# Moving two matmuls behind a Winograd product, and swapping the two column halves of the last one

## The chip, the cores and the metric

The kernel runs on one core of one Trainium2 chip. The metric is device time in microseconds of one launch. Three runs of the kernel before gave 194.7, 194.7 and 194.68 us (median 194.7). A separate execution, taken with the hardware profiler, gave the page and the trace used below; its own time is 194.69 us, and 192.9 us of it lie between its first and its last instruction (the span). The TensorE clock granted in that execution was 1.0 of full speed throughout.

## The reference

A retention layer (linear attention with a decay per head) feeds a two-layer perceptron with the Mish activation, `h * tanh(softplus(h))`.

```python
for t in range(S):                       # B=4, H=8, S=768, D=64
    state = gamma * state + outer(k[:, :, t], v[:, :, t])
    y[:, :, t] = scale * (q[:, :, t] @ state)
x = y.transpose(0, 2, 1, 3).reshape(B * S, H * D)      # 3072 tokens x 512
h = x @ w_in                                            # 512 -> 2048
g = h * tanh(softplus(h))
out = g @ w_out                                         # 2048 -> 512, float32
```

## The kernel before

The recurrence is computed in chunks of 128 tokens; 24 chunks make the 3072 tokens. The chunks are grouped into 11 blocks: block 0 has four chunks (512 tokens), blocks 1 to 10 have two (256 tokens). The order of instructions on each engine is written out by hand, and each engine works through its own list in that order. An instruction starts when the semaphores that it waits for have been reached; what stands behind a waiting instruction on the same engine waits with it. (TensorE has two rows in the trace, PE for the matmuls and PEld for the loads of their stationary operand; a load may run while the matmul before it runs.)

For each of the blocks 4 to 10 the program calls `mixed_in` and then `seven`. Both use a Winograd form: a 2x2 by 2x2 block product with seven block multiplications in place of eight, with sums and differences of blocks made ahead by VectorE (DVE).

`mixed_in` makes the first product, `h = x @ w_in`, transposed: 128 features by 256 tokens at a time, 16 such feature groups. Eight of the groups (0 to 3 and 8 to 11) are made by seven Winograd products; each is a call of `mm` (its matmul is L857) with eight matmuls that move 128 columns. The other eight groups (4 to 7 and 12 to 15) are made plainly; four calls of `plain` (matmul on L877) make two groups each, with eight matmuls that move 256 columns: for each of the two groups four steps over the 512 inputs, which add up in one half of a PSUM bank. Products and plain calls take turns. The results go through

- `kept` (L887), a ScalarE (ACT) copy of a PSUM bank to SBUF,
- `plus` (L892), a DVE addition of a PSUM bank and such a copy,
- `mish` (L868), the ACT activation that writes the block's `g`, 128x512 at a time.

The last part of `mixed_in` is, in order of PE: the product `mm(pf, s(4), b[1][1])`; the third plain call, groups 12 and 13, into the bank of the pool `pxps` (call it po); the product `mm(pa, s(3), t[2])`, "third product" below, which adds onto the bank pa; the fourth plain call, groups 14 and 15, into the bank ph; and `mm(pa, a(1,1), t[3])`, "last product" below, which adds onto the same bank pa once more. Between the last two uses of pa DVE has to read it: `h22 = plus(pa, m5)`. The bank pa can be written again only when that addition has read it.

ACT's last five activations of `mixed_in` are, in this order: h12 (from DVE), po, h22 (from DVE), ph, and pa after the last product.

`seven` makes the block's `out = g @ w_out` for two tiles of 128 tokens, 512 columns in two halves of `hf` = 256, by seven products of eight matmuls each (L951; `mm` of `seven`). Its first product reads groups 0 to 7 of `g`; its second reads groups 12 to 15 and then 8 to 11, of which those of the token half in question are written by the last activation of `mixed_in`, that of pa. `snap` (L957) is an ACT copy from PSUM, `done` (L964 copy, L966 addition) the DVE step that makes a finished part of the output tile; in the last block each `done` is followed at once by a DMA (L968) on the SP queue, in other blocks the stores are issued later.

In `seven` of the last block the last product `mm(.., a(1, 1), t(4))` is cut into two column halves of 128. The half 0 to 127 adds onto the bank px, which by then holds the sum `u3`; it is finished by a copy. The half 128 to 255 is made in a fresh bank pl; it is finished by an addition of the part of `u3` that ACT copied out earlier (`snap(px, ...)`). Before px is written again, the addition `done(1, 1, px, m5)` must have read it.

Of the kernel before, what the change touches and what calls it, by code (L numbers as in the profile page):

```python
# [16 lines left out]
def kernel(  # L17
# [9 lines left out]
    nc = tc.nc  # L27
    B, H, S, D = q.shape
    d_model, d_ff = moe_w_in.shape
    P = 128  # L30
    C = 128
# [8 lines left out]
    NBP = d_model // P  # L40
# [805 lines left out]
    def mixed_in(blk, last):  # L846

        b, t = x_views(blk)
        n = NFB // 4
        gt = gtiles[blk, 0] = gp.tile([P, NFB, 2 * C], FP16, name="g", tag="g", bufs=3)  # L850
        for f in range(NFB):
            gts[blk, f] = gt[:, f]

        def mm(o_ps, w, x, begin=False):
            for f in range(n):
                for k in range(2):
                    nc.tensor.matmul(  # L857
                        o_ps[:, f], w(f // 2, k)[:, f % 2 * P:(f % 2 + 1) * P], x[:, k],
                        start=begin and f == 0 and k == 0, stop=k == 1, skip_group_check=True)

        def a(i, j):
            return lambda h, k: wins[2 * i][h][:, 2 * j + k]

        def s(i):
            return lambda h, k: wsums[h][:, i - 1, k]

        def mish(to, src):
            nc.scalar.activation(to, src, AF.Mish, scale=inv_boost3)  # L868

        def part(i, j):  # L870
            return gt[:, i * 2 * n:i * 2 * n + n, j * C:(j + 1) * C]

        def plain(h_ps, f0):
            for f in range(2):
                w, h = divmod(f0 + f, n)
                for k in range(NBP):
                    nc.tensor.matmul(  # L877
                        h_ps[:, f], wins[w][h // 2][:, k, h % 2 * P:(h % 2 + 1) * P],
                        xts[blk][:, k, :2 * C], start=k == 0, stop=k == NBP - 1)
            return lambda: mish(gt[:, f0:f0 + 2], h_ps)  # L880

        def bank(pool, tag, whole=False):
            return pool.tile([P, 2, 2 * C] if whole else [P, n, C], FP32, name="h_ps", tag=tag)

        def kept(o_ps):
            m = op.tile([P, n, C], FP32, name="hsum", tag="hsum", bufs=6)
            nc.scalar.copy(m, o_ps)  # L887
            return m

        def plus(x, y):  # L890
            m = op.tile([P, n, C], FP32, name="hsum", tag="hsum", bufs=6)
            nc.vector.tensor_tensor(m, x, y, op=ALU.add)  # L892
            return m

        pp = bank(mmps, "mm", True)
        pf = bank(mmps, "mm")
        pa = bank(mmps, "mm")
        mm(pa, a(0, 0), b[0][0], True)
        m1 = kept(pa)
        plain(pp, n)()  # L900
        mm(pf, s(1), t[0], True)
        m5 = kept(pf)
        if not last:
            settle(blk + 1)
            mask_two(blk + 1)
        plain(bank(pxps, "px", True), n + 2)()
        pm = bank(mmps, "mm")
        mm(pm, a(0, 1), b[1][0], True)
        h11 = plus(pm, m1)
        mm(pa, s(2), t[1])  # L910
        u2 = kept(pa)
        mish(part(0, 0), h11)
        mm(pf, s(4), b[1][1])
        h12 = plus(pf, u2)
        mish(part(0, 1), h12)
        plain(bank(pxps, "px", True), 3 * n)()
        mm(pa, s(3), t[2])
        h22 = plus(pa, m5)
        mish(part(1, 1), h22)
        if not last:  # L920
            leave(blk + 1)
        sums_a(blk, 0)
        ph = atps.tile([P, 2, 2, 2 * C], FP32, name="h_ps", tag="at")[:, 0]
        plain(ph, 3 * n + 2)()
        mm(pa, a(1, 1), t[3])
        mish(part(1, 0), pa)
        sums_a(blk, 1)

    def seven(blk, masks, hooks, last):
        n, hf = NFB // 2, d_model // 2  # L930
        px = pxps.tile([P, hf], FP32, name="o_ps", tag="px")
        pb = mmps.tile([P, hf], FP32, name="o_ps", tag="mm")
        osb = [
            op.tile([P, d_model], FP32, name="osb", tag="osb") for _ in range(2)]

        def a(i, j):
            return lambda f: gts[blk, j * n + f][:, i * P:(i + 1) * P]

        def b(i, j):
            return lambda f: wouts[(i * n + f) // FPS][:, f % FPS, j * hf:(j + 1) * hf]  # L940

        def s(i):
            return lambda f: gsums[blk % 2][:, i - 1, f]

        def t(i):
            return lambda f: tmats[(i - 1) // 2][:, (i - 1) % 2, f]

        def mm(o_ps, x, w, first=False, turn=0, part=slice(None), cols=slice(None)):
            for z in range(n)[part]:
                f = (z + turn) % n  # L950
                nc.tensor.matmul(  # L951
                    o_ps[:, cols], x(f), w(f)[:, cols], start=first and z == 0, stop=z == n - 1,
                    skip_group_check=True)

        def snap(o_ps, cols=slice(0, hf)):
            x = op.tile([P, hf], FP32, name="snap", tag="snap", bufs=3)[:, cols]
            nc.scalar.copy(x, o_ps[:, cols])  # L957
            return x

        def done(i, j, o_ps, plus=None, cols=slice(0, hf)):  # L960
            at = slice(j * hf + cols.start, j * hf + cols.stop)
            dst = osb[i][:, at]
            if plus is None:
                nc.vector.tensor_copy(dst, o_ps[:, cols])  # L964
            else:
                nc.vector.tensor_tensor(dst, o_ps[:, cols], plus, op=ALU.add)  # L966
            if last:
                nc.sync.dma_start(out_rows(blk, i)[:, at], dst)  # L968

        def call(fns):  # L970
            for fn, *args in fns:
                fn(*args)

        mm(px, a(0, 0), b(0, 0), True)
        m1 = snap(px)
        mm(pb, a(0, 1), b(1, 0), True, n // 2 if blk >= MIX else 0)
        if blk < ONE:
            sums_b(blk)
            if blk == 1:
                cast_behind(blk, 2)  # L980
            sums_c(blk)
            if blk > 1:
                cast_behind(blk, 3)
            done(0, 0, pb, m1)
            call(masks)
        else:
            done(0, 0, pb, m1)
            if blk == ONE:
                call(masks)
            sums_b(blk)  # L990
            if not tight(blk):
                cast_behind(blk, 2)
                sums_c(blk)
        pe = mmps.tile([P, hf], FP32, name="o_ps", tag="mm")
        alone = blk + 2 >= len(BLOCKS)
        if alone:
            mm(px, s(2), t(2))
            u2 = snap(px)
        mm(pe, s(1), t(1), True)
        m5 = snap(pe)  # L1000
        if not alone:
            mm(px, s(2), t(2))
            u2 = snap(px)
        if blk < ONE:
            mm(pe, s(4), b(1, 1))
            call(hooks[0])
            call(hooks[1])
            done(0, 1, pe, u2)
            mm(px, s(3), t(3), part=slice(0, n // 2))
            call(hooks[2][:1])  # L1010
            mm(px, s(3), t(3), part=slice(n // 2, n))
            pl = mmps.tile([P, hf], FP32, name="o_ps", tag="mm")
            u3 = snap(px)
            done(1, 1, px, m5)
            call(hooks[2][1:])
            mm(pl, a(1, 1), t(4), True)
            done(1, 0, pl, u3)
        else:
            call(hooks[0])
            if tight(blk):  # L1020
                sums_c(blk)
                cast_behind(blk, 3)
            call(hooks[1])
            mm(px, s(3), t(3))
            if last:
                pl = mmps.tile([P, hf], FP32, name="o_ps", tag="mm")
                u3 = snap(px, slice(hf // 2, hf))
            done(1, 1, px, m5)
            call(hooks[2])
            mixes = not last and blk + 1 >= MIX  # L1030
            if mixes:
                x_sums(blk + 1, 0)
            mm(pe, s(4), b(1, 1))
            done(0, 1, pe, u2)
            cols = slice(0, hf // 2 if last else hf)
            mm(px, a(1, 1), t(4), cols=cols)
            done(1, 0, px, cols=cols)
            if last:
                cols = slice(hf // 2, hf)
                mm(pl, a(1, 1), t(4), True, cols=cols)  # L1040
                done(1, 0, pl, u3, cols)
            if mixes:
                x_sums(blk + 1, 1)
        if not last:
            for i in range(2):
                stores.append((1 + i, out_rows(blk, i), osb[i]))
# [344 lines left out]
```

## Time and profile before

| | |
|---|---|
| median of three runs | 194.7 us |
| profiled execution, its own time | 194.69 us |
| its span, first to last instruction | 192.9 us |
| PE busy | 188.0 us, 97% of the span |
| DVE busy | 137.4 us, 71% |
| ACT busy | 104.4 us, 54% |
| POOL busy | 74.0 us, 38% |
| one matmul of 256 columns (L877, L951), start to end | 273 ns |
| one matmul of 128 columns (L857), start to end | 219 ns |
| one load of a stationary operand | 98 ns |
| `mish` L868 from PSUM / from SBUF | 587 / 631 ns |
| `plus` L892 | 691 ns |
| DMA of the last block's 64 KB pieces, issue to landing | 1.6 us |

Matmuls are pipelined: the next one starts long before the one in front has ended, so the pace of a group is read from the starts of groups, not from the duration of one. In the timeline a row is a group of equal instructions that follow each other: start in us from the span's start, us from the first start to the last end, engine, line, operation, tiles and shapes, and in brackets the idle time of the engine before it with what ended it. In the chain of waits, which is followed back from the last instruction, a matmul that had to wait a little still counts as PE.

### The profile page before, as it was taken

To read this page: it belongs to the slowest core of one execution; us is meant where nothing else is said; L and a number is where in the kernel's file an instruction comes from. 1 tells how busy PE (TensorE), PEld (TensorE's weight loads), DVE (VectorE), ACT (ScalarE), POOL (GpSimd) and SP (SyncE) were. 2 spreads that over 40 slices of the span, in tenths; PEclk is the share of its full clock that TensorE was granted. 3 is DMA by queue.
4 is the path that set the end of the run, shared out by engine and by line. 5 is a ranking of instruction groups with operands and counts; after the bars stand their busy time and mean duration, and the time that the engine had idled before them with its cause. 6 is when DMAs were issued, how large, how long until landed. Compare 5 with 4: busy or idle time off the path is not lost.

```text
span 192.9 us, 7199 instructions
## 1 busy us (share of the span) xinstructions
PE 188.0 (97%) x3124; PEld 161.5 (84%) x3124; DVE 137.4 (71%) x273; ACT 104.4 (54%) x193; POOL 74.0 (38%) x100
## 2 busy tenths in 40 slices
PE   7999999999999999999999999999999999999993
PEld 7756478888888888888998998998998989988993
DVE  0787469886977877957985884974884894875462
ACT  3375767263643643554584574664763763763850
POOL 5272000577509648733635625715705800000000
PEclk9999999999999999999999999999999999999999
DMA  5999999998999999999999899999896240201202
GB/s 172 305 308 354 383 388 364 291 322 190 197 238 302 188 243 189 185 276 227 211 197 266 191 195 246 169 211 247 106 235 122 51 130 13 103 0 40 77 27 82
DMA packets 83791, 38.78 MB, mean 201 GB/s; under 512 B 57776, under 2 KB 77872, under 8 KB 83760
## 3 DMA queue, kind: packets, MB, share of 16 engines
q1 hardware_dynamic: 83616, 38.28, 86.3%
q8 instruction: 24, 0.39, 0.9%
q10 hardware_dynamic: 144, 0.05, 0.1%
q14 instruction: 7, 0.06, 0.1%
HBM read 27.31 MB, written 6.29 MB: 174 GB/s over the span
## 4 chain that ended last, share of the span: by engine, by line
PE 94%; DMA 3%; DVE 1%; ACT 1%; issue 0%; SPq 0%
PE o_ps L951 32%; PE h_ps L647 17%; PE h_ps L877 13%; PE h_ps L857 12%; PE o_ps L704 7%; PE y_ps L560 3%; DMA qfirst<-in_q_dram 3%; PE u_ps L488 1%; PE at L481 1%; PE t_ps L256 1%; PE y_ps L382 1%; PE h_ps L629 1%; PE at L452 1%; PE at L336 1%; PE u_ps L354 1%; DVE qk L268 1%
## 5 line engine op out<-in xcount | busy, mean ns | idle before, releaser
L647 PE MATMUL h_ps<-xt,win 128*128 128x256 f16 (+1 forms) x272 | 34.3, 285 | 0.0
L951 PEld LDWEIGHTS <-gsum 128*128 128x128 f16 x320 | 30.3, 98 | 3.9
L647 PEld LDWEIGHTS <-win 128*128 128x128 f16 x272 | 26.4, 98 | 6.5 <-DVE win L213 0.2
L656 ACT ACTIVATE g<-h_ps 128x512 f16<-128x512 f32 x38 | 22.7, 597 | 15.9 <-PE h_ps L647 15.9
L951 PE MATMUL o_ps<-tmat,gsum 128*128 128x256 f16 x240 | 29.8, 273 | 0.0
L877 PE MATMUL h_ps<-xt,win 128*128 128x256 f16 x224 | 29.0, 273 | 0.0
L951 PEld LDWEIGHTS <-g 128*128 128x128 f16 x248 | 23.4, 98 | 2.6
L957 ACT COPY snap<-o_ps 128x256 f32<-128x256 f32 (+1 forms) x33 | 12.2, 369 | 20.1 <-PE o_ps L951 20.1
L966 DVE TENSOR_TENSOR osb<-o_ps,snap 128x256 f32<-128x256 f32 (+1 forms) x33 | 13.8, 417 | 12.8 <-PE o_ps L951 9.2
L877 PEld LDWEIGHTS <-win 128*128 128x128 f16 x224 | 20.7, 98 | 1.9
L868 ACT ACTIVATE g<-h_ps 128x512 f16<-128x512 f32 x35 | 19.9, 587 | 3.3 <-PE h_ps L877 3.3
L887 ACT COPY hsum<-h_ps 128x512 f32<-128x512 f32 x21 | 12.3, 585 | 14.8 <-PE h_ps L857 14.8
L423 POOL TENSOR_TENSOR qk<-qf,qvs 128x512 f16<-128x512 f32 x18 | 19.1, 1061 | 2.0 <-DMA qf<-in_q_dram 2.0
L892 DVE TENSOR_TENSOR hsum<-h_ps,hsum 128x512 f32<-128x512 f32 x21 | 14.5, 691 | 7.4 <-PE h_ps L857 5.2
L426 POOL TENSOR_TENSOR qk<-kf,qvs 128x512 f16<-128x512 f32 x18 | 18.9, 1051 | 1.8 <-DMA kf<-in_k_dram 1.8
L433 POOL TENSOR_TENSOR v<-vf,qvs 128x512 f16<-128x512 f32 x18 | 19.1, 1077 | 1.1 <-DMA vf<-in_v_dram 1.0
L951 PE MATMUL o_ps<-wout,g 128*128 128x256 f16 x160 | 19.1, 273 | 0.0
L1289 POOL COPY summed<-gsum 128x1 f16<-128x1 f16 x7 | 2.9, 421 | 34.2 <-DVE gsum L817 24.5
L857 PE MATMUL h_ps<-xt,wsum 128*128 128x128 f16 x224 | 15.9, 219 | 0.0
L609 ACT CAST xt<-y_ps 128x512 f16<-128x512 f32 x15 | 10.2, 734 | 10.2 <-PE y_ps L560 10.2
L857 PEld LDWEIGHTS <-wsum 128*128 128x128 f16 x224 | 14.0, 98 | 0.3
L868 ACT ACTIVATE g<-hsum 128x512 f16<-128x512 f32 x21 | 13.3, 631 | 1.5 <-DVE hsum L892 1.4
(113 smaller groups left out, 298.6 us busy)
## 6 DMA issues: line engine op xcount, KB each, us to landing
kf<-in_k_dram SPq DMA_DIRECT2D x24, 256.0 KB, 5.4
vf<-in_v_dram SPq DMA_DIRECT2D x24, 256.0 KB, 5.5
out_dram<-osb SPq DMA_DIRECT2D x22, 256.0 KB, 2.8
qf<-in_q_dram SPq DMA_DIRECT2D x20, 256.0 KB, 5.3
wt<-in_moe_w_out_dram SPq DMA_DIRECT2D x6, 512.0 KB, 8.4
wi<-in_moe_w_in_dram SPq DMA_DIRECT2D x4, 512.0 KB, 8.4
wi<-in_moe_w_in_dram SPq DMA_DIRECT2D x2, 1024.0 KB, 11.1
qfirst<-in_q_dram SPq DMA_DIRECT2D x2, 512.0 KB, 4.6
```

Of the source, the lines that this page charges most:

```text
L423: nc.gpsimd.tensor_tensor(in_place(q16.rearrange("p (w x) d -> p w x d", x=2)), by_head(qf), scale_by_head(qs_two[:, heads]), op=ALU.mult)
L426: nc.gpsimd.tensor_tensor(k16.rearrange("p (y w) d -> p w y d", y=2), kf.rearrange("p (w y) d -> p w y d", y=2), boosts.rearrange("p (w y) ...
L433: nc.gpsimd.tensor_tensor(cast[g][2], loaded.pop(g)[2], vs[g % 2].unsqueeze(2).broadcast_to((P, H, D)), op=ALU.mult)
L647: nc.tensor.matmul(h_ps[:, j, cols], wins[s][f // 2][:, bp, f % 2 * P:(f % 2 + 1) * P], xts[blk][:, bp, cols], start=(bp == 0 and at == 0) ...
L656: nc.scalar.activation(gt, h_ps, AF.Mish, scale=inv_boost3)
L704: nc.tensor.matmul(banks[ij][:, t], x(f)[:, t * P:(t + 1) * P], w(f), start=ij in open_banks, stop=f == fs[-1], skip_group_check=True)
L857: nc.tensor.matmul(o_ps[:, f], w(f // 2, k)[:, f % 2 * P:(f % 2 + 1) * P], x[:, k], start=begin and f == 0 and k == 0, stop=k == 1, skip_g ...
L868: nc.scalar.activation(to, src, AF.Mish, scale=inv_boost3)
L877: nc.tensor.matmul(h_ps[:, f], wins[w][h // 2][:, k, h % 2 * P:(h % 2 + 1) * P], xts[blk][:, k, :2 * C], start=k == 0, stop=k == NBP - 1)
L892: nc.vector.tensor_tensor(m, x, y, op=ALU.add)
L951: nc.tensor.matmul(o_ps[:, cols], x(f), w(f)[:, cols], start=first and z == 0, stop=z == n - 1, skip_group_check=True)
L966: nc.vector.tensor_tensor(dst, o_ps[:, cols], plus, op=ALU.add)
```

## The change

In `mixed_in`, `plain` gets an argument that says which of its eight steps to issue. The third plain call issues its first six ahead of the third product and its last two behind it. Its activation is still the one that ACT does before that of h22; DVE's and ACT's lists keep their order. This holds for the blocks 4 to 10.

In `seven` of the last block, the half 128 to 255 of the last product (bank pl, finished by an addition) comes first, and the half 0 to 127 (bank px, finished by a copy) second, with their DVE steps and DMAs in the same new order.

```diff
-        def plain(h_ps, f0):
-            for f in range(2):
+        def plain(h_ps, f0, steps=range(2 * NBP)):
+            for step in steps:
+                f, k = divmod(step, NBP)
                 w, h = divmod(f0 + f, n)
-                for k in range(NBP):
-                    nc.tensor.matmul(
-                        h_ps[:, f], wins[w][h // 2][:, k, h % 2 * P:(h % 2 + 1) * P],
-                        xts[blk][:, k, :2 * C], start=k == 0, stop=k == NBP - 1)
+                nc.tensor.matmul(
+                    h_ps[:, f], wins[w][h // 2][:, k, h % 2 * P:(h % 2 + 1) * P],
+                    xts[blk][:, k, :2 * C], start=k == 0, stop=k == NBP - 1)
             return lambda: mish(gt[:, f0:f0 + 2], h_ps)
...
         mish(part(0, 1), h12)
-        plain(bank(pxps, "px", True), 3 * n)()
+        po = bank(pxps, "px", True)
+        plain(po, 3 * n, range(6))
         mm(pa, s(3), t[2])
         h22 = plus(pa, m5)
+        plain(po, 3 * n, range(6, 2 * NBP))()
         mish(part(1, 1), h22)
...
             mm(pe, s(4), b(1, 1))
             done(0, 1, pe, u2)
-            cols = slice(0, hf // 2 if last else hf)
-            mm(px, a(1, 1), t(4), cols=cols)
-            done(1, 0, px, cols=cols)
             if last:
                 cols = slice(hf // 2, hf)
                 mm(pl, a(1, 1), t(4), True, cols=cols)
                 done(1, 0, pl, u3, cols)
+            cols = slice(0, hf // 2 if last else hf)
+            mm(px, a(1, 1), t(4), cols=cols)
+            done(1, 0, px, cols=cols)
```

## The prediction

> **What bounds the kernel now.** I read the page first, then the timeline of the last `mixed_in` and `seven` engine by engine. The page's head and its chain of waits:
>
> ```profile
> span 192.9 us, 7199 instructions
> ...
> PE 94%; DMA 3%; DVE 1%; ACT 1%; issue 0%; SPq 0%
> ```
>
> TensorE sets the end almost throughout: only PE time that goes away, or the tail behind the last matmul, counts. Small waits of PE are hidden in that 94%; they show only in the starts of groups. The PE timeline of block 10, from the first Winograd product beside `po` onward:
>
> ```profile
> 179.46 0.61 PE L857 MATMUL h_ps<-xt,win 128*128 128x128 f16 x8
> 179.91 1.06 PE L857 MATMUL h_ps<-xt,wsum 128*128 128x128 f16 x16
> 180.80 1.04 PE L877 MATMUL h_ps<-xt,win 128*128 128x256 f16 x8
> 181.67 0.61 PE L857 MATMUL h_ps<-xt,wsum 128*128 128x128 f16 x8
> 182.12 1.04 PE L877 MATMUL h_ps<-xt,win 128*128 128x256 f16 x8
> 183.06 0.55 PE L857 MATMUL h_ps<-xt,win 128*128 128x128 f16 x7
> ```
>
> Eight matmuls of 256 columns (po, 180.80) take 0.87 us to the next group's start, so 0.109 each; eight of 128 (third product, 181.67) take 0.45, so 0.056 each. The fourth plain call (182.12) takes 0.94: its successor, the last product, starts 0.07 late. DVE says why:
>
> ```profile
> 181.22 0.69 DVE L892 TENSOR_TENSOR hsum<-h_ps,hsum 128x512 f32<-128x512 f32 x1 [0.36 <-ACT hsum L887]
> 182.32 0.69 DVE L892 TENSOR_TENSOR hsum<-h_ps,hsum 128x512 f32<-128x512 f32 x1 [0.40 <-PE h_ps L857]
> ```
>
> The second row is h22. It starts 0.04 after the end of the third product (181.67 + 0.61 = 182.28), ends at 183.01, and 0.05 later PE writes the same bank. The seven blocks agree; from the start of the fourth plain call to that of the last product they show 0.95, 0.94, 0.94, 0.95, 0.95, 0.94, 0.94 us (blocks 4 to 10: 97.76 to 98.71, 111.91 to 112.85, 126.05 to 126.99, 140.26 to 141.21, 154.30 to 155.25, 168.35 to 169.29, 182.12 to 183.06), together 6.61 against 7 x 0.873 = 6.11.
>
> ACT in the same stretch, po, h22, ph and pa:
>
> ```profile
> 182.49 0.58 ACT L868 ACTIVATE g<-h_ps 128x512 f16<-128x512 f32 x1
> 183.04 0.63 ACT L868 ACTIVATE g<-hsum 128x512 f16<-128x512 f32 x1
> 183.58 1.06 ACT L868 ACTIVATE g<-h_ps 128x512 f16<-128x512 f32 x2
> ```
>
> They run without a gap, 0.54 apart, and the whole row is 0.7 behind PE: the activation of po starts at 182.49, though po's matmuls ended at 181.84.
>
> The tail, PE and then DVE:
>
> ```profile
> 187.88 1.04 PE L951 MATMUL o_ps<-wout,gsum 128*128 128x256 f16 x8
> 188.85 1.05 PE L951 MATMUL o_ps<-tmat,g 128*128 128x128 f16 x16
> ```
>
> ```profile
> 188.37 0.42 DVE L966 TENSOR_TENSOR osb<-o_ps,snap 128x256 f32<-128x256 f32 x1 [1.24 <-ACT snap L957]
> 188.95 0.42 DVE L966 TENSOR_TENSOR osb<-o_ps,snap 128x256 f32<-128x256 f32 x1 [0.15 <-PE o_ps L951]
> 189.49 0.29 DVE L964 COPY osb<-o_ps 128x128 f32<-128x128 f32 x1
> 189.94 0.29 DVE L966 TENSOR_TENSOR osb<-o_ps,snap 128x128 f32<-128x128 f32 x1 [0.16 <-PE o_ps L951]
> ```
>
> The eight matmuls from 187.88 should be over at 188.75 by pace; the next start at 188.85, 0.06 after `done(1, 1, px, m5)` has read px (188.37 + 0.42 = 188.79). So PE loses 0.10 there.
>
> **The change, part by part.** No instruction is added or removed on any engine, no DMA and no pool's tile; ACT, POOL and SP keep their lists, DVE too up to the last two instructions of all.
>
> *The two matmuls, block 10 as the example.* The third product is reached after six steps, at 180.80 + 6 x 0.109 = 181.45. It needs the bank pa read by the copy of u2, which ends at 181.19: no wait, 0.2 to spare. Its last matmul starts 7 x 0.056 later, at 181.84, and ends 0.22 later, at 182.06; h22 starts at 182.10 (DVE is free from 181.91), ends at 182.79 and lets PE write at 182.84. PE meanwhile does the two remaining steps (181.90 to 182.12) and the fourth plain call from 182.12, as before, and wants the bank at 182.12 + 0.87 = 182.99. The wait is gone with 0.15 to spare. Gain: 0.07 in each of seven blocks, **0.49 us**; bounds 0 and 0.08 a block.
>
> *What is late next.* po is complete later: its last matmul starts at 182.01 and ends at 182.28, so its activation could start at 182.32. It starts at 182.49 anyway, behind that of h12: hidden with 0.17 to spare. If that cover were gone, each 0.1 would be passed on through the gapless row to the activation of pa. There the margin is thin. `seven`'s second product needs it at its fifth step, the thirteenth matmul of L951; in block 9:
>
> ```profile
> 169.68 1.35 PEld L951 LDWEIGHTS <-g 128*128 128x128 f16 x13
> 169.74 1.47 PE L951 MATMUL o_ps<-wout,g 128*128 128x256 f16 x12
> 169.81 1.06 ACT L868 ACTIVATE g<-h_ps 128x512 f16<-128x512 f32 x2
> ```
>
> The activations end at 170.87; with the 0.04 seen above the thirteenth load may start at 170.91. It did at 170.93 (169.68 + 1.35 - 0.10), ahead of its matmul at 169.74 + 12 x 0.109 = 171.05. Now PE comes 0.07 earlier and ACT doesn't: the load would go at 170.86 and must wait for 170.91, its matmul is due at 170.98. The first load and matmul of this group lie 0.06 apart, as do those of the gapless groups of 128 columns: that gives 170.97, just in time. If the matmul had to wait for all 0.098 of the load it would be 171.01, a loss of 0.03 a block, 0.21 in all. I take 0, as the spacing of 0.06 is what full pace shows, and keep both ends.
>
> [...]
>
> Other waits of PE have more room than the 0.07 by which it comes earlier: the sums of the second half (DVE, L813, ends 185.38; its load is due at 185.15 + 4 x 0.109 = 185.59), and the snap of px (ACT, 184.64 + 0.37 = 185.01, px is written again at 185.25).
>
> *The swap in the last block.* The half in pl needs no reader of px; it starts at 188.75 and ends at 188.75 + 7 x 0.056 + 0.22 = 189.36, its addition runs from 189.40 (DVE's `done(0, 1)` ends at 189.37) to 189.69. The half in px starts at 189.20, long after 188.79, ends at 189.81; its copy runs from 189.84 to 190.13, against 190.23 before. Copy and addition cost the same 0.29, so the exchange of the two brings nothing by itself. The SP queue issued its last store at 190.30 in 0.40; its last three would now be ready 0.3 and 0.4 apart, with 0.33 to 0.38 for an issue, so that queueing costs at most some 0.04. Gain **0.10 us**; bounds 0 and 0.12.
>
> **Sum.** 0.49 + 0.10 = 0.59. The profiled execution took 194.69 us in all (span 192.9 and 1.8 around it), as good as the median of 194.7. Forecast 194.69 - 0.59 = **194.1 us**, its own range 193.95 to 194.3.
>
> **Rivals.**
>
> 1. *The gain is handed to ACT.* PE is faster by 0.07 only up to the thirteenth matmul of `seven`. For it: ACT's row has no gap and the margin is 0.01. Against it: the 0.06 spacing. With 0.03 lost a block and half the tail's gain: 194.69 - 0.28 - 0.05 = 194.36; with all of it lost, 194.6.
> 2. *The wait wasn't h22's.* If PE pays the 0.07 for the turn from the fourth plain call to the last product, only the tail's 0.10 is left: 194.59. For it: every block shows the same value. Against it: the same turn elsewhere (178.59 to 179.46) costs nothing, and DVE's end lies 0.05 ahead of the start each time.
> 3. *Slower: coming back to an open bank costs PE.* The change adds a break in each plain call: out of po, back into it, then on to ph. Turns cost something somewhere: the eight matmuls from 173.83 in block 9 are followed by 64x64 ones at 174.81, 0.98 later, 0.11 over their pace. At 0.10 for leaving and for coming back: 14 x 0.10 = 1.4, so 194.69 + 1.4 - 0.59 = 195.5; it decides from 0.08 a block (no gain left). Against it: turns between 128 and 256 columns at full array width cost nothing in any row above.
> 4. *The small matmuls change their pace.* The stage of 64x64 matmuls in the blocks 4 to 8 takes 1.23, 1.24, 1.31, 1.13 and 1.14 us for 120, 128, 128, 120 and 128 matmuls: 10.2, 9.7, 10.2, 9.4, 8.9 ns each, for no reason that the rows show. All at 10.2 adds 0.34 (194.44), all at 8.9 takes off 0.5 (193.6).
>
> **Chances.** Forecast 0.62; rival 1 0.17; 2 0.06; 3 0.07; 4 0.08. Runs of one kernel lie within 0.02 us here; about 0.2% (0.39 us) is what can be told from no change, so faster means below 194.31. That is the forecast, a quarter of rival 1 and half of rival 4: 0.70. Slower is rival 3: 0.07. The rest, 0.23, is the same. The range: 193.9 (a part of rival 4's gain) to 194.65 (rivals 1 and 2), which leaves out some 0.12.
>
> **What would show it.** Right: in all seven blocks the last product starts 0.87 after the fourth plain call, h22 some 0.22 earlier against the start of po, the activation of po still gapless behind that of h12, the thirteenth matmul of `seven` in pace; in the tail a single row of sixteen 128-column matmuls that starts 0.87 after the eight before, and a last DVE row that ends 0.6 earlier in the span. Wrong: a gap ahead of the activation of po, the 0.07 turning up within the first sixteen L951 matmuls, or more than 1.32 us from the start of po to that of the fourth plain call.

## The result and the profile after

The changed kernel took 194.19 us (median of ten runs, 194.11 to 195.39) against 194.66 for the kernel before (ten runs, 194.55 to 194.82); the ratio is 0.998, 95% interval 0.9971 to 0.9989. The profiled executions stand at 194.15 against 194.69 us. So it is faster by about half a microsecond, a quarter of a per cent; 194.1 was forecast. One execution in the experiments below, the profiled one of `only_swap`, took 484.61 us where the ten others of that kernel took 194.57 to 195.87, so another execution of it, `swap_look`, is read in its place.

The span is 192.4 us now, where it was 192.9, and the chain of waits has the same shares as before, PE 94% and DMA 3% at its head. Nothing in the shares tells the two kernels apart. The timeline does. Block 10, kernel after, all engines, weight loads left out (start in us, duration, engine, line):

```profile
180.31 0.82 PE L877 MATMUL h_ps<-xt,win 128*128 128x256 f16 x6
...
180.97 0.61 PE L857 MATMUL h_ps<-xt,wsum 128*128 128x128 f16 x8
...
181.41 1.26 PE L877 MATMUL h_ps<-xt,win 128*128 128x256 f16 x10
181.46 0.63 ACT L868 ACTIVATE g<-hsum 128x512 f16<-128x512 f32 x1 [0.23 <-DVE hsum L892]
181.62 0.69 DVE L892 TENSOR_TENSOR hsum<-h_ps,hsum 128x512 f32<-128x512 f32 x1 [0.18 <-PE h_ps L857]
182.00 0.58 ACT L868 ACTIVATE g<-h_ps 128x512 f16<-128x512 f32 x1
...
182.48 0.62 ACT L868 ACTIVATE g<-hsum 128x512 f16<-128x512 f32 x1
182.51 0.61 PE L857 MATMUL h_ps<-xt,win 128*128 128x128 f16 x8
...
182.95 1.91 PE L953 MATMUL o_ps<-wout,g 128*128 128x256 f16 x16
183.00 1.07 ACT L868 ACTIVATE g<-h_ps 128x512 f16<-128x512 f32 x2
```

The ten matmuls from 181.41 (the two moved ones and the fourth plain call) take 1.10 us to the last product at 182.51: 10 x 0.109 = 1.09, no wait left. h22 (DVE, 181.62) now ends at 182.31, 0.20 before PE writes its bank. From po's start to the first matmul of `seven`, PE takes 2.64 us where it took 2.71 (180.80 to 183.51). The other six blocks show 2.64 too, against 2.71 before.

The tail of the kernel after, PE and DVE from the timeline, then the SP queue's last three stores:

```profile
187.32 1.04 PE L953 MATMUL o_ps<-wout,gsum 128*128 128x256 f16 x8
...
188.19 1.06 PE L953 MATMUL o_ps<-tmat,g 128*128 128x128 f16 x16
188.39 0.74 DVE L968 TENSOR_TENSOR osb<-o_ps,snap 128x256 f32<-128x256 f32 x2
189.29 0.29 DVE L966 COPY osb<-o_ps 128x128 f32<-128x128 f32 x1 [0.15 <-PE o_ps L953]
```

```profile
188.85 0.33 SPq L970 DMA_DIRECT2D out_dram<-osb  x1
189.27 0.38 SPq L970 DMA_DIRECT2D out_dram<-osb  x1
189.75 0.40 SPq L970 DMA_DIRECT2D out_dram<-osb  x1
```

and the same three stores of the kernel before:

```profile
189.40 0.33 SPq L968 DMA_DIRECT2D out_dram<-osb  x1
189.83 0.38 SPq L968 DMA_DIRECT2D out_dram<-osb  x1
190.30 0.40 SPq L968 DMA_DIRECT2D out_dram<-osb  x1
```

On PE the swap did what it should: the last row starts 0.87 after the one in front (188.19 - 187.32) where it took 0.97, and DVE's last step ends at 189.58, 0.65 earlier than before. But the last store is issued at 189.75, 0.17 after its data were there, and only 0.55 earlier than before. The three issues keep the distances 0.42 and 0.48 that they had before (0.43 and 0.47): the queue's own pace sets them, counted from the store of `done(0, 1)`, and that store waits for a product which the swap doesn't touch. Between two issues SP has a wait instruction for the data of the next one; ahead of the last store the trace has it from 189.70 to 189.72, after the end of the issue in front (189.65) and long after the data (189.58), so it isn't the data that it waits for. A tenth was won on PE and lost on SP.

The 0.55 at the last store is made up so: block 4 already starts 0.07 earlier (92.39 against 92.46), in work that the change doesn't touch, which is a difference between two executions; the seven blocks give 7 x 0.07; the tail nothing.

### The profile page after: what moved, and what is told of

Same layout as the page of the kernel before. It is cut to its first block, busy times and chain, and to the rows that moved or that the text cites. A ratio compares the mean times of both kernels' runs of the same rounds, so it can differ in the third digit from the quotient of the medians.

```text
span 192.4 us, 7199 instructions
## 1 busy us (share of the span) xinstructions
PE 186.7 (97%) x3124; PEld 160.9 (84%) x3124; DVE 138.3 (72%) x273; ACT 103.9 (54%) x193; POOL 74.0 (38%) x100
## 4 chain that ended last, share of the span: by engine, by line
PE 94%; DMA 3%; DVE 1%; ACT 1%; issue 0%; SPq 0%
PE o_ps L953 32%; PE h_ps L647 17%; PE h_ps L877 13%; PE h_ps L857 11%; PE o_ps L704 7%; PE y_ps L560 3%; DMA qfirst<-in_q_dram 3%; PE u_ps L488 1%; PE at L481 1%; PE t_ps L256 1%; PE y_ps L382 1%; PE h_ps L629 1%; PE at L452 1%; PE at L336 1%; PE u_ps L354 1%; DVE qk L268 1%
## 5 line engine op out<-in xcount | busy, mean ns | idle before, releaser
L609 ACT CAST xt<-y_ps 128x512 f16<-128x512 f32 x15 | 10.2, 733 | 10.2 <-PE y_ps L560 10.2
```

## The experiments

Each is an edit of the changed kernel unless it says otherwise. Theory A is that all of the gain is h22's wait, seven times, and that the swap's tenth is lost to the pace of the SP queue.

**The two parts alone.** `only_move` takes the changed kernel with the two halves of the last product back in the old order; `only_swap`, and `swap_look` for its trace, take the kernel before with only the halves swapped.

```diff
 # only_move, against the changed kernel
-            if last:
-                cols = slice(hf // 2, hf)
-                mm(pl, a(1, 1), t(4), True, cols=cols)
-                done(1, 0, pl, u3, cols)
             cols = slice(0, hf // 2 if last else hf)
             mm(px, a(1, 1), t(4), cols=cols)
             done(1, 0, px, cols=cols)
+            if last:
+                cols = slice(hf // 2, hf)
+                mm(pl, a(1, 1), t(4), True, cols=cols)
+                done(1, 0, pl, u3, cols)
```

> The two matmuls moved, the tail as before. Theory A (the whole gain comes from the seven blocks, because the last store waits for the SP queue's pace of 0.42 and 0.48 us per issue and not for the last DVE step): 194.2, the same as the change within 0.05; DVE's last row ends some 0.1 later than in the change, the last store is issued at the same time, 189.75. Theory B (the swap is worth its 0.10 of PE time): 194.29, last store issued at 189.85.

Measured: 194.21 us, ratio to before 0.998 (0.9971 to 0.9989). The move alone has the whole gain. In its trace the last DVE step ends at 189.68, 0.10 later than in the change, and the last store is issued at 189.74, as there (189.75).

> The halves swapped, the two matmuls not moved. Theory A: 194.66 as before the change; PE's last row starts 0.10 earlier than before (188.75) and DVE ends near 190.13, but the last store is issued at 190.30 as before. Theory B: 194.56, last store at 190.20.

Measured: 194.68 us, ratio 1.0007 (0.9995 to 1.0019): nothing in the medians, though the interval would just allow a tenth of a microsecond, so the trace has to decide. The one read here is that of `swap_look` (194.66 us):

> As only_swap, for its trace. Theory A: the last product's row starts 0.87 after the row before it (0.97 before the change), the last store is issued 2.42 us after the start of that row before, as before the change. Theory B: 2.32.

The tail in that trace, PE and DVE, then the last two stores:

```profile
187.83 1.04 PE L951 MATMUL o_ps<-wout,gsum 128*128 128x256 f16 x8
...
188.71 1.06 PE L951 MATMUL o_ps<-tmat,g 128*128 128x128 f16 x16
...
189.80 0.29 DVE L964 COPY osb<-o_ps 128x128 f32<-128x128 f32 x1 [0.15 <-PE o_ps L951]
```

```profile
189.78 0.38 SPq L968 DMA_DIRECT2D out_dram<-osb  x1
190.26 0.40 SPq L968 DMA_DIRECT2D out_dram<-osb  x1
```

PE's wait is gone (0.88), the copy ends at 190.09, yet the last store goes out at 190.26: 2.43 after 187.83, against 2.42 before (187.88 to 190.30) and 2.43 in the changed kernel (187.32 to 189.75). Theory A holds in all three traces.

**Taking the SP queue out of the way.** `tail_act` issues the last store from ACT's queue; `tail_one` sends both halves in one store, after the copy.

```diff
 # tail_act
-        def done(i, j, o_ps, plus=None, cols=slice(0, hf)):
+        def done(i, j, o_ps, plus=None, cols=slice(0, hf), queue=None):
...
-                nc.sync.dma_start(out_rows(blk, i)[:, at], dst)
+                (queue or nc.sync).dma_start(out_rows(blk, i)[:, at], dst)
...
-            done(1, 0, px, cols=cols)
+            done(1, 0, px, cols=cols, queue=nc.scalar if last else None)
 # tail_one
-        def done(i, j, o_ps, plus=None, cols=slice(0, hf)):
+        def done(i, j, o_ps, plus=None, cols=slice(0, hf), store=None):
...
-            if last:
-                nc.sync.dma_start(out_rows(blk, i)[:, at], dst)
+            if last and store is None:
+                store = at
+            if last and store:
+                nc.sync.dma_start(out_rows(blk, i)[:, store], osb[i][:, store])
...
-                done(1, 0, pl, u3, cols)
+                done(1, 0, pl, u3, cols, False)
...
-            done(1, 0, px, cols=cols)
+            done(1, 0, px, cols=cols, store=slice(0, hf) if last else None)
```

> The change, but the last store (half 0 to 127) is issued on ACT's queue, which is idle, not behind the two stores on SP. Theory A: it is issued 0.04 after the copy ends, some 189.62 where it was 189.75, so 0.10 to 0.13 faster than the change, 194.08. Rival (what counts is the store's way to landing, or ACT's issue is slower): 194.2 or more.

Measured: 194.08 us, ratio to before 0.997 (0.9961 to 0.9979). From the timeline of `tail_act`:

```profile
189.43 0.29 DVE L966 COPY osb<-o_ps 128x128 f32<-128x128 f32 x1 [0.16 <-PE o_ps L953]
189.75 0.38 ACTq L970 DMA_DIRECT2D out_dram<-osb  x1
```

The store goes out 0.03 after the copy's end (189.72), where it waited 0.17 on SP. This execution ran 0.14 later as a whole (its last 256-column product starts at 187.46), so the issue stands 2.29 after that start.

> The change, but the two halves of the last product leave in one store of 128 KB after the copy, not in two of 64 KB. Theory A: SP is free from 189.18, issues at 189.62 in 0.33 where it did at 189.75 in 0.40; landing 1.7 where it was 1.6 to 1.7: 0.1 to 0.2 faster than the change, 194.0 to 194.1. Rival (the larger transfer costs what the queue gives): 194.2.

Measured: 193.99 us, ratio 0.9969 (0.9957 to 0.998), the fastest version here. The copy and the store behind it, two views of `tail_one`:

```profile
189.40 0.29 DVE L966 COPY osb<-o_ps 128x128 f32<-128x128 f32 x1 [0.16 <-PE o_ps L953]
```

```profile
189.72 0.33 SPq L972 DMA_DIRECT2D out_dram<-osb  x1
```

With one store fewer the queue is free when the copy ends at 189.69, and the store goes out 2.29 after the start of the last 256-column product (187.43), as in `tail_act`: 0.14 earlier than in the change. The issue itself takes 0.33 where the 64 KB pieces take 0.38 to 0.40, but that brings nothing, since landing, counted from the start of the issue, is 1.7 us for both sizes. The rest of the 0.20 lies behind the landing. In the change the last store lands at 191.42 and the span ends at 192.37, 0.95 later; in `tail_act` it is 0.94, here 0.83 (191.42 to 192.25). SP ends each of these programs with five waits, one behind the other. In the change the landing of the last store releases the third of them, and two more follow, 0.06 each; here it releases the fifth. Counted from the start of the last 256-column product, the span of `tail_one` ends 0.23 earlier than that of the change: 0.14 from the queue, 0.11 from this row of waits, less some 0.02 that landing takes longer.

With the queue out of the way the swap should at last be worth its tenth. `move_one` is `tail_one` with the halves in the old order, so that both end with the same row of waits (0.83 and 0.84 from landing to the end of the span):

> The two matmuls moved, the last product's halves in the old order, and one store for both halves. Theory A (the swap's 0.10 us of PE time is real and was lost to the pace of the SP queue): with one store the queue is free, so this is 0.10 slower than the same with the halves swapped: 194.09 against 193.99, the last store issued 2.39 us after the start of the last 256-column product, against 2.29. Rival (the swap brings nothing in any case): equal within 0.03.

> As tail_one, beside the run without the swap on one chip: 193.99; last store issued 2.29 us after the start of the last 256-column product.

Measured side by side: 194.11 without the swap and 194.02 with it. The last store is issued 2.39 after the start of the last 256-column product (187.35 to 189.74) and 2.29 (187.41 to 189.70). The medians differ by 0.09, as expected, though the intervals of the two ratios overlap (0.996 to 0.9982 and 0.9959 to 0.9978); the traces carry this point.

**How many matmuls behind the third product.** The changed kernel with one, four and six of the eight in place of two:

```diff
-        plain(po, 3 * n, range(6))
+        plain(po, 3 * n, range(2))                      # behind_6; range(4): behind_4; range(7): behind_1
...
-        plain(po, 3 * n, range(6, 2 * NBP))()
+        plain(po, 3 * n, range(2, 2 * NBP))()
```

> One matmul of the third plain call behind the third product instead of two (halves as in the change). Theory A (the wait was that for h22, and two matmuls leave 0.15 us to spare): one leaves 0.04, the step from the fourth plain call to the last product stays 0.87: 194.2, as the change. If the room is smaller than told, up to 0.07 a block comes back: up to 194.6.

Measured: 194.21 us. One is enough; in its trace the last product starts 0.98 after the nine matmuls in front of it do, 9 x 0.109, so no wait is left.

> Four matmuls behind the third product. It is then reached 0.44 us after the start of po, and the copy of u2 out of the same bank ends 0.39 after it, 0.44 with the 0.05 to PE. Theory A: 0 to 0.05 a block lost, 194.2 to 194.55; the activation of po starts as in the change, since po's last matmul ends at the same time. Theory C (each return to an open bank costs PE, whatever their place): as the change, 194.2.

Measured: 194.18 us, ratio 0.9981 (0.9972 to 0.999), as with two. In its trace the third product starts 0.45 after po (180.32 to 180.77), the twelve matmuls behind it 0.44 later (181.21), and the last product 1.31 after those (182.52): 4 x 0.109, 8 x 0.056 and 12 x 0.109, all within 0.01. Theory A allowed for a loss of 0 to 0.05, so the time doesn't tell theories A and C apart; the rows show that neither leaving the open bank nor coming back to it costs PE more than that 0.01.

> Six matmuls behind the third product. It is reached 0.22 after the start of po and must wait for the copy of u2 until 0.44: 0.22 lost in each of seven blocks, 1.5 in all: 195.7, with a gap between po's first two matmuls and the third product. If the copy of u2 is not what bounds how early the product may come: 194.2.

Measured: 195.69 us, ratio 1.0056 (1.0043 to 1.0069). From the timeline of `behind_6`:

```profile
181.42 0.59 ACT L887 COPY hsum<-h_ps 128x512 f32<-128x512 f32 x1 [0.35 <-PE h_ps L857]
...
181.62 0.38 PE L877 MATMUL h_ps<-xt,win 128*128 128x256 f16 x2
...
182.06 0.61 PE L857 MATMUL h_ps<-xt,wsum 128*128 128x128 f16 x8
```

Two matmuls take 0.22, so the third product could start at 181.84. It starts at 182.06, 0.05 after ACT's copy of u2 out of its bank ends (182.01): 0.22 lost in block 10 and about as much in the blocks 5 to 9, 0.17 in block 4, 1.5 us together, as worked out beforehand. So the place has two edges: too late, and h22 holds up the last product; too early, and u2 holds up the third. From one to four matmuls lie between them; five were not run. The 1.5 us are accounted for by that wait alone, so coming back to the open bank costs PE nothing here either; what leaving it costs would be hidden in the wait in this run.

**ACT's order and its room.** `act_h22_first` lets ACT do h22 ahead of po:

```diff
-        plain(po, 3 * n, range(6, 2 * NBP))()
+        late = plain(po, 3 * n, range(6, 2 * NBP))
         mish(part(1, 1), h22)
+        late()
```

> The change, with ACT doing the activation of h22 ahead of that of po. ACT then idles from the end of its step for h12 until h22 is there (182.31 plus 0.04 in block 10, 0.35 later than it now starts po), and the activations of ph and pa come 0.35 later. Theory A (the second product of seven needs that of pa with some 0.06 to spare): 0.29 lost in each of seven blocks, 2.0 in all, 196.2; the thirteenth L951-type matmul of each block waits. Rival (ACT has room of 0.35 or more there): 194.2.

Measured: 198.07 us, ratio 1.0177 (1.0163 to 1.0191). Slower as expected, but by 3.9 us over the change, not 2.0. The wait is not where it was expected. PE's waits by what they were for (total us, times, longest), and the end of block 10 in the timeline of this kernel:

```profile
PE o_ps L954 <- ACT g L868: 2.7, 7, 0.4
```

```profile
185.86 0.61 PE L857 MATMUL h_ps<-xt,win 128*128 128x128 f16 x8
186.24 1.55 ACT L868 ACTIVATE g<-h_ps 128x512 f16<-128x512 f32 x3
...
186.87 1.91 PE L954 MATMUL o_ps<-wout,g 128*128 128x256 f16 x16 [0.39 <-ACT g L868]
```

Not the thirteenth matmul of `seven` waits but the first: due at 185.86 + 0.45 = 186.31, it starts at 186.87, 0.56 late, and 7 x 0.56 = 3.9. (The list of waits counts only the time in which PE is idle, 0.39 of the 0.56.) The groups 0 to 7 of `g` that it reads were written by 185.45. But it writes the bank px, and px is the bank that po had (both are the one buffer of `pxps`); it is free when ACT has read po, 186.24 + 0.58 = 186.82. The expectation looked for the reader of `g` and missed the owner of the bank.

`act_late` was to measure the room of the thirteenth matmul:

```diff
+        nc.scalar.copy(seen, warm)
         mish(part(1, 0), pa)
```

> The change, with one small ACT copy (128x1, some 0.16 us) put between the activations of ph and of pa in each mixed block. It delays the activation of pa alone. If the thirteenth matmul of seven has the room of 0.06 to 0.1 us that the trace of the change shows, 0.06 to 0.1 is lost in each of seven blocks: 194.6 to 194.9. If there is more room than 0.16: 194.2.

Measured: 194.18 us, as the change. The timeline of `act_late`, ACT from the small copy on:

```profile
183.43 0.19 ACT L928 COPY seen<-warm 128x1 f32<-128x1 f32 x1
183.51 0.61 ACT L868 ACTIVATE g<-h_ps 128x512 f16<-128x512 f32 x1
```

The small copy is 0.19 long, but the next activation starts 0.08 after the copy's start, so the two overlap; that of pa ends at 184.12, 1.21 after the start of `seven` on PE (182.91), where it was 1.12 (184.07 against 182.95). A delay of 0.09, not the 0.16 that was meant, costs nothing, and the weight loads (PEld) and matmuls show why. The thirteenth load of `seven` in `act_late`, then PE:

```profile
184.17 0.10 PEld L954 LDWEIGHTS <-g 128*128 128x128 f16 x1
```

```profile
182.91 1.91 PE L954 MATMUL o_ps<-wout,g 128*128 128x256 f16 x16
...
184.65 1.58 PE L954 MATMUL o_ps<-tmat,gsum 128*128 128x256 f16 x13
```

In the change this load starts 1.20 after `seven` does, 0.08 after the end of pa's activation (from the unrounded trace, as what follows). In `act_late` it had to wait: it starts 1.26 after `seven`, 0.05 after the end of the activation. Its matmul starts at 184.22, 12 x 0.109 after the first one and so in pace, 0.05 behind the start of a load that takes 0.10; the next product starts in pace too (182.91 + 16 x 0.109 = 184.65). So the room for the load was some 0.03 and is used up; that for the matmul was larger, and how much of it is left beyond this delay no run shows.

## Why the prediction was right

- *The wait for h22, 0.49 us.* Right in mechanism, place and size: the rows show 0.07 gone in each of seven blocks, `only_move` gives 0.45 between the medians, and `behind_1` bears out the 0.15 of room (one matmul gives back 0.11 of it, and no wait returns).
- *The cover for po.* Its activation still follows that of h12 (181.46, then 182.00) without a gap: hidden, as told.
- *What is late next.* The sum was right (nothing lost), one reading behind it was not. ACT's row was not without a gap before: the step from po's activation to that of h22 was 0.55 (182.49 to 183.04) and is 0.48 now (182.00 to 182.48). It had been waiting for h22, which ended at 183.01. So ACT gained the same 0.07 as PE, the activation of pa keeps its distance to `seven` (1.13 before, 1.12 after), and the margin that rival 1 lived on never shrank. `act_late` shows that another 0.09 would have been free, and settles the choice between the two ends of this step: with the load held up to 0.05 ahead of its matmul, the matmul was still in pace, so it need not wait for all 0.098 of its load, and the loss of 0.03 a block does not occur. What the step left out is the bank px: ACT has read po at 182.58 now, and `seven` writes that bank at 182.95, which leaves 0.32 after the 0.05 to PE where it was 0.40. `act_h22_first` shows what happens when that is gone.
- *The swap, 0.10 us.* This is the term of the sum that failed. The prediction put queueing on SP at "at most some 0.04", from issue durations of 0.33 to 0.38. The distance from one issue to the next is longer than the duration, 0.42 and 0.48, and before the change the last two stores already sat close behind one another: the last one went out 0.07 after its data were there, where 0.03 is enough with a free queue (`move_one`, 189.71 to 189.74). The true value at the last store was 0, as the trace of `swap_look` shows; `move_one` and `tail_one_again` show that the tenth is there once the queue is free.
- *Rival 2* (not h22) falls: the same turn costs nothing after. *Rival 3* (leaving and coming back to an open bank) falls by the rows of the change (6, 8 and 10 matmuls take 0.66, 0.44 and 1.10, their plain pace) and by `behind_4`. *Rival 4*: the stage of 64x64 matmuls takes 1.24, 1.24, 1.30, 1.13 and 1.14 us in the blocks 4 to 8, within 0.01 of before; the change didn't touch it. Its prices were misread: the rows show 120, 120, 128, 120 and 120 such matmuls, so 10.3, 10.3, 10.2, 9.5 and 9.5 ns each, and the two ends are some 0.2 more and 0.3 less, not 0.34 and 0.5.
- *The noise.* Three runs lay within 0.02 us; the ten runs of the kernel before lie between 194.55 and 194.82. The gain of 0.47 is clear of that, a term of 0.10 is hardly to be seen in medians alone, which is why the tail is read from the traces.

So the gain is 0.49, not 0.59, and the measured 0.47 lies beside it; the range held because it had room for a swap that brings nothing.

Moving one store to ACT's queue (`tail_act`) brought 0.11 us between the medians and left landing at 1.7 us. Behind the last matmul nothing covers those 0.11 us: they are the end of the kernel.

## What to carry to other kernels

A wait shorter than one instruction (0.07 us here, beside matmuls of 0.22) didn't show in the chain of waits or in busy shares; it shows as the start of one group against the start of the next, compared with the same turn elsewhere. When a matmul group waits for another engine's read of its bank, a few independent matmuls moved between the two were worth just the wait (0.07 us in each of seven blocks), and there was a window for how many (one, two and four took 194.2 us, six 195.69): work out both edges, and look at who owns the bank next as well as at who reads the data. At the very end of a kernel count the distance between DMA issues on one queue (0.42 and 0.48 us here), not their duration (0.33 and 0.38), before paying for an earlier last result. One store fewer was worth more here (0.20 us between the medians of the change and `tail_one`), and not only on the queue (0.14 there, 0.11 behind the landing): look also at what the program still does after the last store has landed.

## What the runs showed of the hardware

- The SP queue issued back-to-back stores 0.42 and 0.48 us apart, though the issues are recorded as 0.33 and 0.38 long; a 128 KB store was issued in 0.33 and a 64 KB one in 0.38 to 0.40, and both landed after 1.6 to 1.7 us.
- From the landing of the last store to the end of the span it took 0.94 to 0.95 us with four stores in the last stretch and 0.83 to 0.84 with three; two waits of SP less stood behind the landing.
- A matmul started in pace 0.05 after the start of its own load, which took 0.10 (`act_late`).
- ACT took in a 0.19 us copy between two activations at a cost of 0.08 to 0.09 (the step from the one to the other was 0.48 in the change, 1.07 less the 0.59 of the second, and 0.56 with the copy).
- An accumulation that is interrupted after six or four matmuls (the change, `behind_4`) for another of eight cost PE no more than some 0.01 us on leaving and on coming back: in the change the 6, 8 and 10 matmuls took 0.66, 0.44 and 1.10, in `behind_4` the 4, 8 and 12 took 0.45, 0.44 and 1.31, beside paces of 0.109 and 0.056 for one.
